# Attention with a token MLP on one core: a planner's settings, a per-window table, ramp jobs with their own priorities, an earlier constant and a scaling in two groups

## The chip, the cores and the metric

The kernel runs on one core of a Trainium2 chip. Its time is device microseconds of that core, taken as the median of several runs. A separate execution was recorded by the hardware profiler; its trace gives a span from the first to the last instruction. Five engines each work through their own list of instructions in order: PE (TensorE, matrix products), ACT (ScalarE), DVE (VectorE), POOL (GpSimd) and SP, which here only starts transfers. Matrix products land in PSUM, 8 banks of 128 x 512 float32.

## The reference

The input x has 2,048 rows of 640 numbers. It is normalised twice: once for the attention, and once more ahead of the MLP.

```python
x = A_x
xn = _layernorm(x)
s = _A_ref(xn, A_wqkv, A_wo)                  # attention, 32 heads of 20
g = _silu(_B_ref(xn, B_w1, B_b1, B_w2, B_b2)) # MLP over the rows (tokens)
return x + s * g

# _A_ref: q, k, v = split(xn @ wqkv); p = softmax(q k^T * 20**-0.5); o = p v; o @ wo
# _B_ref: h = _layernorm(xn); u = gelu(h^T-contraction over rows with w1, 1536 wide, + b1);
#         y = u^T-contraction with w2 (back to 2048) + b2
```

The largest part is the softmax: 32 heads x 2,048 x 2,048 exponentials.

## The kernel before

**Units and passes.** The heads are taken four at a time (eight groups G), the query columns 512 at a time (four blocks). One group and one block make a pass: 16 chunks of 128 keys, four heads each, 64 units of 128 keys x 512 queries. There are 32 passes, the last in two halves. A unit's life: PE makes its scores in a PSUM bank (L1313, four heads side by side in 32-row groups), an engine turns them into weights in SBUF, and PE multiplies the weights with V (L1429), adding to the pass's accumulator bank. The row sums come along as a column of ones in V. When a pass is full, DVE transposes the accumulator (L1557), takes reciprocals (L1560), scales (L1565), and the result goes out by a transfer.

**Two ways to an exponential.** Most units go through ACT: one instruction (L1343) takes two or three banks at once, 128x1024 or 128x1536, and writes bf16 to a ring of 20 slots, pt_sb. The rest go through DVE in tiles of four units (one chunk, four heads). DVE writes an integer whose bits, read as bf16, are a rough exponential (L1354). Three more copies, each with a constant added, are averaged by PE through four differently scaled V operands (v_sb, and vs_sb from L793), which evens the error out. A copy is made by DVE (L1407, 128x2048) or, for the fourth one, by a transfer issued by POOL that adds a constant tile kc_sb onto the first copy in place once PE has used it (L1378). These are the adding transfers. `x_ok` decides between the two, when the third copy is being made:

```python
def x_ok(d):
    if "kc" not in done or pr.xpipe > pr.T["dve"] + self.XQ:
        return False
    return d["q"] > a_cur[0] or a_left(d["q"]) >= self.XLEFT
```

The six banks of ACT form two groups of three. In `do_st`, ACT may lend the third bank of a group to a DVE unit: that exponential then covers two units instead of three. DVE can also use the spare bank 7.

**The planner.** The order is not written by hand. When the program is built, `schedule` plays all engines forward with a cost for each instruction and always emits the ready candidate with the lowest priority number on the engine that can start first. `Prog` keeps the book: `_add` reckons starts, ends and waits, also those of transfers (XISSUE, XMOVE, XTAIL for the adding ones). The result is a fixed list per engine, with waits on semaphores; each list is executed strictly in that order. Class attributes of `_Kern` steer the choices: how much DVE backlog still allows lending (LEND, LENDF), how long a job may wait (LATE, JOBF), the number of ACT units left in a pass below which DVE takes no more (D_GUARD), when an adding transfer is allowed (XLEFT, XQ), where MLP matmuls are spread (MLP_A, MLP_B). `tune` may set them anew every 16 units from the table PLAN and the value lists OPTS; in this kernel PLAN is empty.

**The ramp.** The first 40 to 60 us do what later passes rely on. Rows arrive in blocks of 128 (x), DVE takes statistics two blocks at a time (L557, L559, L564, L568), POOL raises the variance to the power -1/2 (L571), and DVE applies it (L575). The first four blocks are transposed on PE (L626) and evicted by ACT and DVE (L633, L636), the other twelve by transposing transfers from SP (L613). PE then makes k and q of the first group (L660) and V of the first eight heads (L773), evicted by L1140, L1141, L1143 and L1144. The second normalisation is only a further scaling of the same rows: DVE computes its variance from the first (L586, L588, L590), POOL takes a power of 16 columns (L592), and DVE scales all 16 blocks (L595). Bank jobs of the ramp are chosen in `activate_` by readiness and priority. Idle time on PE may be filled with dummy products: L1456 (`emit_warm`) before the first PV product, then L1446 (`emit_fill`), which adds zeros to the accumulator and is drawn only if the planner's own measure of PE's activity is low.

**Around it.** Later q and k are projected in columns of 32 (L675), stored to HBM scratch through three staging slots qs_sb (L705) and loaded back per group (L744). MLP products (L675; row pieces L683 ride beside a score product) and their evictions (L850) fill gaps. At the end the output projection (L992, L997), its product with the gate (L1007, L1775), the residual add (L1033, and for the last two blocks L1777, the first of them on POOL) and the stores (L1042, L1784) remain.

Of the kernel before, what the change touches and what calls it, by code (L numbers as in the profile page):

```python
# [39 lines left out]
class Prog:  # L40
# [7 lines left out]
    XISSUE, XMOVE, XTAIL = 950.0, 2900.0, 4600.0  # L48
# [42 lines left out]
    def _add(self, eng, ceng, fn, reads, writes, name, extra_req=(), cost=100.0, tail=None):  # L91
# [55 lines left out]
        elif ceng not in self.COMPUTE:  # L147
# [3 lines left out]
            if tail is not None:  # L151
                self.T[eng] = start + cost
                self.pipe = max(self.pipe, start) + cost
                t.fin = self.pipe - cost + tail
            else:
                self.T[eng] = start + 450.0
                self.pipe = max(self.pipe, start + 600.0) + cost
                t.fin = self.pipe + (1200.0 if self.pipe < 2500.0 else 2800.0 if cost > 800.0 else 1400.0)
# [125 lines left out]
class _Kern:  # L284
# [16 lines left out]
    D_GUARD = 20  # L301
    MLP_A, MLP_B = 2.6, 24.0
    QK_LEAD = 6.0
    SLACK, MINJ = 0.0, 640.0
    ROOM = 6
    ROWM, ROWP, ROWN = 4, 2, 400
    lastrow = None
    LENDH, LEND1, JLATE = 0.0, 9999.0, 0.0
    LENDF = 1800.0
    MERGE = False  # L310
    OPM = 1
    KLEAD = 300.0
    KPRIO = 22.4
    RAMPEND = ('qk0_1_3', 'qk0_0_1')
    RLEND = 0
    DRDY = 'lnp14'
# [3 lines left out]
    JOBF = 4  # L320
    LONE, DLEAD, DRIDE = True, 0.0, 700.0
# [8 lines left out]
    ACTP = 30.0  # L330
# [3 lines left out]
    OTA, OTD = 24.6, 0.1  # L334
    XLEFT, XQ = 18, 4000.0
# [9 lines left out]
        ("DRIDE", (400.0, 150.0, 700.0)),  # L345
        ("LEND", (1800.0, 1300.0, 2400.0, 700.0, 0.0)),
# [3 lines left out]
        ("LONE", (False, True)),  # L350
# [3 lines left out]
        ("FGAP", (0.0, 40.0, 150.0)),  # L354
# [3 lines left out]
    PLAN = ()  # L358
    PARTS = (3, 1)
# [78 lines left out]
    def schedule(self):  # L438
# [111 lines left out]
        def ln_steps(b0, nb):  # L550
# [10 lines left out]
            for b in bl:  # L561
# [10 lines left out]
                          [sw, S_("mhalf")], sr, f"{nm}pow", 1020.0))  # L572
# [8 lines left out]
        def r2_steps():  # L581
            steps = []
            mvs = [S_(f"mv{b}") for b in range(NB)]
            srs = [S_(f"rstd{b}") for b in range(NB)]
            sw = S_("r2w")
            steps.append(("dve", lambda e: e.tensor_tensor(st(5, 0, NB), st(2, 0, NB), st(2, 0, NB), ALU.mult), srs,  # L586
                          [sw], "r2a", 100.0))
            steps.append(("dve", lambda e: e.tensor_tensor(st(5, 0, NB), st(5, 0, NB), st(1, 0, NB), ALU.mult),  # L588
                          [sw] + mvs, [sw], "r2b", 100.0))
            steps.append(("dve", lambda e: e.tensor_scalar(st(5, 0, NB), st(5, 0, NB), self.EPS, None, ALU.add), [sw],  # L590
                          [sw], "r2c", 100.0))
            steps.append(("pool", lambda e: e.tensor_tensor(st(6, 0, NB), st(5, 0, NB), mhalf(NB), ALU.pow),  # L592
                          [sw, S_("mhalf")], [S_("r2")], "r2d", 2900.0))
            for b in range(NB):
# [157 lines left out]
        def wp_step(w):  # L752
# [3 lines left out]
                     f"wp0_{w}", 430.0),  # L756
                    ("tag", f"wp0_{w}")]

        def v_steps(b, half):
            def make(bk):  # L760
                steps = []
                c0, n = (0, 160) if half == 0 else (160, 480)
# [1511 lines left out]
```

## Time and profile before

| what | value |
|---|---|
| median of 3 runs | 758.12 us (757.94 to 758.52) |
| the profiled execution | 761.36 us, of which span 759.5 us |
| ACT busy | 727.9 us (96%) |
| PE busy | 715.1 us (94%) |
| DVE busy | 684.8 us (90%) |
| POOL busy | 104.6 us (14%) |
| exponentials on ACT (L1343) | 682 |
| adding transfers (L1378) | 94, 512 KB each, median 5.9 us from issue to landing |
| mean granted PE clock | 0.993 |

Busy time counts an instruction from its start to its end. On ACT and DVE a following instruction starts some tenths of a microsecond before the previous one's end, so that a mean duration is longer than the distance between two of them; the busy time of a group counts overlapping stretches once. What follows "|" last in a group is the time its engine stood still just before these instructions, and the work whose end let them start. The clock column shows what share of full speed PE was granted.

### The profile page before, as it was taken

What the parts mean: (1) busy time and instruction counts of PE and PEld (TensorE: products, weight loads), DVE (VectorE), ACT (ScalarE), POOL (GpSimd) and SP (SyncE); (2) the same over time, 40 slices, a digit from 0 to 9 for tenths busy, and PEclk for the clock granted to TensorE, in tenths of its full rate; (3) what the DMA queues carried; (4) which work ended last, traced back from release to release, by engine and by line L of the source; (5) the groups of instructions that cost most, each with busy time, mean ns of one, the idle gap of its engine ahead of it and who ended that gap; (6) DMA issues with size and microseconds to landing.
All of it is one profiled execution on the core that took longest, in us unless ns stands there. A gap on an engine that the chain in (4) does not pass through costs nothing.

```text
span 759.5 us, 23600 instructions
## 1 busy us (share of the span) xinstructions
PE 715.1 (94%) x10485; PEld 240.1 (32%) x10485; DVE 684.8 (90%) x1247; ACT 727.9 (96%) x708; POOL 104.6 (14%) x118
## 2 busy tenths in 40 slices
PE   8889999999999999999999999999999999999997
PEld 7332222222232323233232322332332332332233
DVE  8789889989898988898998898999999999999996
ACT  6879999999999999999999999999999999999994
POOL 4301111011111100000000011120111111001100
PEclk9899999999999999999999999999999999999999
DMA  9749754556787727364313586746679885395522
GB/s 242 139 104 127 152 102 84 104 106 123 140 144 144 151 43 165 79 134 68 68 48 64 117 171 116 149 80 150 121 129 173 150 171 112 63 234 131 107 63 71
DMA packets 133274, 91.95 MB, mean 121 GB/s; under 512 B 80676, under 2 KB 119972, under 8 KB 133124
## 3 DMA queue, kind: packets, MB, share of 16 engines
q0 software_dynamic: 13536, 49.29, 34.9%
q1 hardware_dynamic: 119636, 41.15, 24.9%
q8 instruction: 82, 1.34, 0.7%
q14 instruction: 20, 0.16, 0.1%
HBM read 26.37 MB, written 10.22 MB: 48 GB/s over the span
## 4 chain that ended last, share of the span: by engine, by line
ACT 70%; PE 20%; DVE 6%; DMA 3%; issue 0%; SPq 0%; POOL 0%; DVEq 0%
ACT pt_sb L1343 69%; PE ps_all L1429 6%; PE ps_all L1313 6%; PE ps_all L675 5%; DMA dt_sb<-kc_sb 1%; DVE dt_sb L1354 1%; ACT zt_sb L871 1%; PE ps_all L660 1%; PE ps_all L992 1%; DVE dt_sb L1407 1%; ACT zt_sb L876 1%; DMA regA<-in_A_x_dram 1%; DVE regC L575 1%; DMA xnT_sb<-regC 0%; DVE tr_sb L1557 0%; DVE regC L595 0%
## 5 line engine op out<-in xcount | busy, mean ns | idle before, releaser
L1343 ACT ACTIVATE pt_sb<-ps_all 128x1024 bf16<-128x1024 f32 (+1 forms) x682 | 708.9, 1224 | 10.9 <-PE ps_all L1313 7.5
L1354 DVE TENSOR_SCALAR dt_sb<-ps_all 128x512 uint16<-128x512 f32 x504 | 334.7, 681 | 42.6 <-PE ps_all L1313 20.2
L1313 PE MATMUL ps_all<-qk_sb 32*128 32x512 bf16 (+1 forms) x2128 | 271.1, 377 | 27.7 <-ACT pt_sb L1343 23.4
L1407 DVE TENSOR_SCALAR dt_sb<-dt_sb 128x2048 uint16<-128x2048 uint16 x284 | 186.5, 685 | 2.4 <-PE ps_all L1429 0.4
L1378 POOL DMA_DIRECT2D dt_sb<-kc_sb x94 | 87.5, 944 | 609.3 <-PE ps_all L1429 395.8
L1313 PEld LDWEIGHTS ps_all<-qk_sb 32*128 32x128 bf16 x2128 | 68.5, 91 | 282.4 <-ACT pt_sb L1343 213.6
L1429 PE MATMUL ps_all<-dt_sb,vs_sb 128*21 128x512 bf16 (+1 forms) x1560 | 135.4, 377 | 1.8 <-DMA dt_sb<-kc_sb 1.4
L1429 PE MATMUL ps_all<-pt_sb,v_sb 128*21 128x512 bf16 (+1 forms) x1608 | 127.1, 374 | 3.0 <-DVE v_sb L1141 2.0
L675 PE MATMUL ps_all<-regC,regA 128*32 128x128 bf16 (+1 forms) x1440 | 66.5, 295 | 0.8 <-DVE qs_sb L1141 0.6
L675 PE MATMUL ps_all<-regB,regA 128*32 128x512 bf16 (+1 forms) x1460 | 66.1, 297 | 0.1
L1429 PE MATMUL ps_all<-dt_sb,v_sb 128*21 128x512 bf16 (+1 forms) x520 | 49.6, 376 | 3.4 <-DVE tr_sb L1557 3.2
L1429 PEld LDWEIGHTS ps_all<-dt_sb,vs_sb 128*21 128x21 bf16 x1560 | 35.4, 90 | 54.0 <-issue 30.7
L1429 PEld LDWEIGHTS ps_all<-pt_sb,v_sb 128*21 128x21 bf16 x1608 | 30.6, 90 | 48.8 <-issue 35.7
L675 PE MATMUL ps_all<-xnT_sb,wqk_sb 128*32 128x512 bf16 x612 | 45.3, 382 | 0.0
L683 PE MATMUL ps_all<-regC,regA 32*128 32x512 bf16 x96 | 36.9, 385 | 0.0
L675 PEld LDWEIGHTS ps_all<-regB,regA 128*32 128x32 bf16 x1460 | 27.5, 96 | 24.5 <-issue 12.9
L675 PEld LDWEIGHTS ps_all<-regC,regA 128*32 128x32 bf16 x1440 | 27.1, 96 | 23.3 <-issue 12.0
L683 PE MATMUL ps_all<-regB,regA 32*128 32x512 bf16 x76 | 29.2, 385 | 0.0
L992 PE MATMUL ps_all<-wv_sb,xnT_sb 128*128 128x128 bf16 (+1 forms) x160 | 28.6, 301 | 0.0
L1557 DVE STREAM_TRANSPOSE tr_sb<-ps_all 128x512 f32<-128x512 f32 x31 | 21.9, 707 | 0.9 <-PE ps_all L1429 0.9
L675 PE MATMUL ps_all<-wv_sb,xnT_sb 128*32 128x480 bf16 x312 | 22.2, 384 | 0.0
L1429 PEld LDWEIGHTS ps_all<-dt_sb,v_sb 128*21 128x21 bf16 x520 | 13.2, 91 | 23.9 <-issue 11.1
(93 smaller groups left out, 383.8 us busy)
## 6 DMA issues: line engine op xcount, KB each, us to landing
dt_sb<-kc_sb POOLq DMA_DIRECT2D x94, 512.0 KB, 5.9
regA<-in_B_w_dram SPq DMA_DIRECT2D x6, 1024.0 KB
regA<-in_B_w_dram SPq DMA_DIRECT2D x8, 768.0 KB
qk_sb<-qk_scratch_dram SPq DMA_DIRECT2D x56, 80.0 KB
qk_scratch_dram<-qs_sb SPq DMA_DIRECT2D x32, 128.0 KB
regA<-in_A_x_dram SPq DMA_DIRECT2D x6, 640.0 KB
ok_scratch_dram<-on_sb SPq DMA_DIRECT2D x96, 20.0 KB
out_dram<-regC SPq DMA_DIRECT2D x3, 640.0 KB
```

Of the source, the lines that this page charges most:

```text
L575: steps.append(("dve", lambda e, b=b: e.tensor_scalar(regC[:, b, :], regA[:, b, :], st_sb[:, 0, b:b + 1], st_sb[:, 2, b:b + 1], ALU.subtra ...
L660: steps.append(("pe", lambda e, dc=dc, lhsT=lhsT: e.matmul(ps(bk, n), lhsT, xnT_sb[:, dc, tb * 512 + c0:tb * 512 + c0 + n], start=(dc == 0 ...
L675: fns.append(lambda e, c=c, e_=e_: e.matmul(oc(c, e_), lhsT[:, c:e_], rhs, start=start, stop=stop, tile_position=(0, c)))
L683: row = lambda g: (lambda e: e.matmul(oc(0, 128), lhsT[32 * g:32 * g + 32, :], rhs[32 * g:32 * g + 32, :], start=False, stop=False, tile_p ...
L992: steps.append(("pe", lambda e, c=c: e.matmul(ap, oT_sb[:, c, b * 128:(b + 1) * 128], wo_ap[:, c, c0:c0 + n], start=(opens and c == 0), st ...
L1313: t = pr.pe(lambda e, outp=outp, lhsT=lhsT, rhs=rhs, g=g: e.matmul(outp, lhsT, rhs, start=True, stop=True, tile_position=(32 * g, 0)), rea ...
L1343: tk = pr.act(lambda e: e.activation(outp, inp, AF.Exp, scale=math.log(2.0) / 128.0), reads=[bank_slot[b] for b in banks[:n]], writes=[S_( ...
L1354: tk = pr.dve(lambda e: e.tensor_scalar(w, src, WOFF, 0.0, ALU.add, ALU.max), reads=[bank_slot[bk]], writes=[S_(f"dt{d['tl'][0]}_{g}")], n ...
L1378: t = pr.xdma(lambda e: e.dma_start(dst, kc_sb[:, :, :], accum_op=ALU.add), [S_("kc")] + sl_, sl_, f"dX{d['q']}_{d['c']}")
L1407: tk = pr.dve(lambda e: e.tensor_scalar(dst, src, dk, None, ALU.add), reads=[S_(f"dt{b}_{g}") for b in inb for g in range(4)], writes=[S_( ...
L1429: pr.pe(lambda e: e.matmul(outp, lhsT, rhs, start=(k == 0), stop=last, tile_position=(0, 32 * g)), reads=reads, writes=[bank_slot[AB]], na ...
L1557: steps.append(("dve", lambda e: e.transpose(tr_sb[:, :], ps(AB)), [bank_slot[AB]], [S_("tr")], f"epT{q}", 632.0))
```

## The change

The class attributes are set anew. PLAN gets a table of 122 rows, one for each 16 units, which pick values from OPTS. The reckoned tail of an adding transfer goes from 4.6 to 5.6 us, and every other transfer that starts after 45 us is reckoned 1.5 us longer. The memset of kc_sb loses its requirement, so it is issued ahead of the first power. The second scaling is split into blocks 0 to 7 and 8 to 15. V tiles of the ramp come in groups of one to three blocks (VGRP) with priorities of their own (JP). The residual add of the tail stays on DVE for both last blocks; narrow output products come in pairs (OPM). The diff, with repeated or minor places cut:

```diff
-    XISSUE, XMOVE, XTAIL = 950.0, 2900.0, 4600.0
+    XISSUE, XMOVE, XTAIL = 950.0, 2900.0, 5600.0
...
-                t.fin = self.pipe - cost + tail
+                t.fin = self.pipe - cost + tail + (1500.0 if start > 45000.0 else 0.0)
...
-    D_GUARD = 20
-    MLP_A, MLP_B = 2.6, 24.0
-    QK_LEAD = 6.0
+    D_GUARD = 8
+    MLP_A, MLP_B = 2.0, 25.0
+    QK_LEAD = 7.0
...
-    LENDF = 1800.0
-    OPM = 1
+    LENDF = 2400.0
+    OPM = 2
...
-    RAMPEND = ('qk0_1_3', 'qk0_0_1')
-    RLEND = 0
-    DRDY = 'lnp14'
+    RESP = 39.0
+    R2N = 8
+    XE = ((2,), (2,))
+    JP = {'k0_0': 26.95, 'v0_0': 21.16, 'q0_0': 25.64, 'v0_14': 19.07, 'k0_1a': 25.82, 'v0_13': 30.17, 'v0_8': 19.61}
+    VGRP = ((0, 2), (2, 2), (4, 3), (7, 1), (8, 3), (11, 1), (12, 3), (15, 1))
+    RAMPEND = ('v0_14', 'qk0_0_1')
+    RLEND = 1
+    DRDY = 'qk0_1_3'
...
-    JOBF = 4
-    LONE, DLEAD, DRIDE = True, 0.0, 700.0
+    JOBF = 6
+    LONE, DLEAD, DRIDE = False, 0.0, 700.0
...
-    ACTP = 30.0
+    ACTP = 22.0
...
-    OTA, OTD = 24.6, 0.1
-    XLEFT, XQ = 18, 4000.0
+    OTA, OTD = 25.0, 0.16
+    XLEFT, XQ = 20, 4000.0
...
-    PLAN = ()
-    PARTS = (3, 1)
+    PLAN = (
+        "000000000000000", "000000000000000", "000000000000000", "000000000000000", "100000000000000", "100000000000000",
+        "000030000000000", "000000000000000", "000000000000000", "000030000000000", "000000000000001", "000000000000000",
...
+    )
+    PARTS = (1,)
...
-        def r2_steps():
+        def r2_steps(b0, nb, tag):
...
-            steps.append(("pool", lambda e: e.tensor_tensor(st(6, 0, NB), st(5, 0, NB), mhalf(NB), ALU.pow),
-                          [sw, S_("mhalf")], [S_("r2")], "r2d", 2900.0))
-            for b in range(NB):
+            steps.append(("pool", lambda e: e.tensor_tensor(st(6, b0, nb), st(5, b0, nb), mhalf(nb), ALU.pow),
+                          [sw, S_("mhalf")], [sr], "r2d", 400.0 + 156.0 * nb))
+            for b in bl:
...
-        def v_steps(b, half):
+        def v_steps(b, half, nb=2):
...
-        add_job("r2", r2_steps(), sum((xtag(gb) for gb in range(4)), ()), 43.0)
+        if self.R2N:
+            add_job("r2a", r2_steps(0, self.R2N, "h_a"), sum((xtag(gb) for gb in range((self.R2N + 3) // 4)), ()), 43.0)
+        add_job("r2", r2_steps(self.R2N, NB - self.R2N, "h_all"), (("h_a",) if self.R2N else ()) + sum((xtag(gb) for gb in range(4)), ()), 43.0)
...
         add_job("kc", [("pool", lambda e: e.memset(kc_sb[:, :, :], int(self.DK[3])), [], [S_("kc")], "kc", 1800.0), ("tag", "kc")],
-                ("lnp14",), 43.0)
+                (), 43.0)
...
-            for b in range(4 * gb, 4 * gb + 4, 2):
-                add_bank_job(f"v0_{b}", v_steps(b, 0), xt + ((f"qk0_1_{gb}",) if gb else ("qk0_0_0", "qk0_1_0")), self.VPRIO + gb)
+            for b, nb in self.VGRP:
+                if (b + nb - 1) // 4 == gb:
+                    need = xt + (xtag(gb - 1) if b // 4 < gb else ())
+                    add_bank_job(f"v0_{b}", v_steps(b, 0, nb), need + ((f"qk0_1_{gb}",) if gb else ("qk0_0_0", "qk0_1_0")), self.VPRIO + gb)
...
-            steps.append(("pool" if i < 1 else "dve", lambda e: e.tensor_tensor(g0, g0, regA[:, b, 0:512], ALU.add),
+            steps.append(("dve", lambda e: e.tensor_tensor(g0, g0, regA[:, b, 0:512], ALU.add),
...
-                  (80.0 if pr.T["pe"] < 4500.0 else 0.0), w=81.0)
+                  (80.0 if pr.T["pe"] < 5600.0 else 0.0), w=81.0)
...
-                        c.append((99.0, max(T, 1000.0), emit_warm))
+                        c.append((99.0, max(T, 1185.0), emit_warm))
```

## The prediction

> **What bounds the kernel now.** I read four views in this order. First the page's engine row.
>
> ```profile
> PE 715.1 (94%) x10485; PEld 240.1 (32%) x10485; DVE 684.8 (90%) x1247; ACT 727.9 (96%) x708; POOL 104.6 (14%) x118
> ```
>
> Busy times of pipelined work include tails, so PE at 94% is not yet the bound. ACT has 759.5 - 727.9 = 31.6 us without work; DVE has 74.7. Second, the chain of work that ended last (70% of it runs through ACT), and busy time by stretch, which tells where those 31.6 us lie:
>
> ```profile
> ACT 70%; PE 20%; DVE 6%; DMA 3%; issue 0%; SPq 0%; POOL 0%; DVEq 0%
> ```
>
> ```profile
> 0.00:20.00 20.00, 17.48 (x202) 14.23 (x206) 17.02 (x63) 12.06 (x16) 8.40 (x16) 1.00 0.94 236
> 20.00:40.00 20.00, 17.55 (x148) 6.08 (x141) 13.94 (x45) 15.53 (x12) 6.88 (x6) 0.83 0.76 155
> 40.00:60.00 20.00, 17.85 (x199) 6.69 (x197) 17.80 (x41) 17.23 (x18) 2.56 (x2) 1.00 0.42 94
> 60.00:100.00 40.00, 37.94 (x496) 11.00 (x488) 34.23 (x61) 37.19 (x37) 3.70 (x5) 0.96 0.77 129
> 100.00:150.00 50.00, 49.44 (x675) 14.34 (x671) 48.13 (x83) 49.93 (x51) 7.52 (x8) 1.00 0.53 99
> ...
> 500.00:550.00 50.00, 47.24 (x747) 15.03 (x744) 49.09 (x87) 49.38 (x51) 5.99 (x8) 1.00 0.60 120
> ...
> 740.00:759.50 19.50, 13.99 (x201) 6.77 (x201) 13.51 (x29) 8.63 (x8) 1.15 (x1) 0.99 0.20 69
> ```
>
> Columns: length; PE, PEld, DVE, ACT, POOL busy with counts; granted clock; DMA share; GB/s. ACT misses 15.2 us before 60 (7.9 + 4.5 + 2.8), 2.8 from 60 to 100, about 2.7 from 100 to 740, and 10.9 at the end. So from 60 to 740 the time is ACT's queue of exponentials, back to back, and a change pays in two ways: less in that queue, or less idle at the start, at 90-97 and at the end.
>
> Third, the costliest groups with shapes kept apart: the prices.
>
> ```profile
> L1343 ACT ACTIVATE pt_sb<-ps_all 128x1024 bf16<-128x1024 f32 x500 | 483.8, 1115 | 3.7 <-PE ps_all L1313 2.7 <-PE ps_all L683 0.2
> L1354 DVE TENSOR_SCALAR dt_sb<-ps_all 128x512 uint16<-128x512 f32 x504 | 334.7, 681 | 42.6 <-PE ps_all L1313 20.2 <-PE ps_all L683 19.2
> L1343 ACT ACTIVATE pt_sb<-ps_all 128x1536 bf16<-128x1536 f32 x181 | 265.7, 1531 | 7.2 <-PE ps_all L1313 4.8 <-PE ps_all L1429 2.2
> L1407 DVE TENSOR_SCALAR dt_sb<-dt_sb 128x2048 uint16<-128x2048 uint16 x284 | 186.5, 685 | 2.4 <-PE ps_all L1429 0.4
> L1378 POOL DMA_DIRECT2D dt_sb<-kc_sb x94 | 87.5, 944 | 609.3 <-PE ps_all L1429 395.8 <-DVE dt_sb L1407 127.9 <-DVE zt_sb L850 21.6
> ```
>
> Fourth, the timeline of the places where ACT stood: around 28 us, and near the end.
>
> ```profile
> 28.13 1.81 POOL L1611 MEMSET kc_sb<- 128x2048 uint16 x1
> 28.22 1.90 DVE L575 TENSOR_SCALAR regC<-regA,st_sb 128x640 bf16<-128x640 bf16 x1 [0.81 <-POOL st_sb L571]
> ...
> 752.73 1.15 POOL L1777 TENSOR_TENSOR regC<-regC,regA 128x512 bf16<-128x512 bf16 x1 [20.51 <-DVE regC L1775]
> 752.87 1.35 DVE L1033 TENSOR_TENSOR regC<-regC,regA 128x640 bf16<-128x640 bf16 x1
> ```
>
> Twice a DVE instruction that alone takes 0.4 to 0.5 us ran as long as a POOL instruction beside it.
>
> **The change, part by part.** A planner writes every queue's order when the program is built, so the built instruction lists of both kernels tell what moved; no time is taken from the planner.
>
> *The mix of units.* A unit is one 128x512 block of scores. ACT's exponentials go from 500 of two units, 181 of three and 1 of one (1,544 units) to 514 and 168 (1,532). There are 682 instructions both times, so only columns go: 12 x (1,531 - 1,115 = 416 ns) = **-5.0 us** on the queue that sets 60 to 740. The 12 units move to DVE: 12 x 334.7/504 = 8.0 us. The adding transfers (L1378) fall from 94 to 64, so L1407 rises from 284 to 323: 39 x 186.5/284 = 25.6 us. Other DVE edits nearly cancel: 7 products of 256 columns for 14 of 128 save about 0.7, one residual add comes from POOL for 0.4, V evictions 0.4 more. DVE goes from 684.8 to about 718 us. In 60 to 740 it has 57.4 us free (680 less the sum of its stretches), so this lies beside ACT with some 24 left; a DVE stall then delays a borrowed bank (L1354), hence the score matmuls, hence ACT. The stretches 100-150 and 500-550 show DVE at 48.1 and 49.1 of 50 while ACT lost 0.1 and 0.6. Scaled from the latter, 680 us at such density lose 8.4; from the former, 1.0. I take **+1.5**, since only some stretches become so dense.
>
> *PE.* 56 more column pieces, 48 more matmuls with DVE weights, 12 fewer with ACT's and 36 fewer zero fillers are 56/4 = 14 more passes of four; a pass adds 0.22 us (groups of 8 span 0.61, of 4 span 0.39): 3.1 us, against 44 without work. The 56 row pieces that vanish started with a score matmul and cost nothing. PE: 0.
>
> *The constant.* The memset of kc_sb goes from behind the last of the eight power instructions to ahead of the first, behind v_ones, which ends at 2.76 + 2.85 = 5.61. POOL's first power (5.86, 0.72 long) now waits until 5.6 + 1.8 = 7.4, so DVE's first L575, at 6.92 today, starts at 8.1; behind it wait the 20 transposes on PE, the first projections and the first exponential (11.01). **+1.2 us** at the start, unhidden. In return the 1.90 us L575 becomes 0.4, and 0.8 of waiting around it shrinks.
>
> *Ramp jobs and second scaling.* V evictions get groups and priorities; 8 of the 16 scalings (L595, 0.3 us apart) move ahead of the last V work. DVE's list up to the last L575 carries 0.9 us more work and 1.2 of late start, and sheds the 1.5 at 28.2 and about 1.2 of waits. It comes out even, but ten scalings no longer stand in one block (39.19 to 42.2) ahead of a V eviction, for which PE, the exponential buffers and ACT waited. ACT's waits between 30 and 44 are 1.05 + 0.56 + 2.72 + 2.21 = 6.5 us. Bounds: 0 regained, or all 6.5; I take **-4**, because the list puts nearly every V eviction before the second group. The second power (128x16: 2.90; 128x2: 0.69, so 128x8 about 1.6) stands ahead of two first powers, but 2.6 us of DVE work stand before the next apply: hidden by 0.2; without that cover it costs at most 1.6.
>
> *A rule against this part: the clock.* In the ramp's first pass fillers drop from 60 matmuls to 24. The clock stood at half from 32.2 to 39.1 and from 93.7 to 97.1:
>
> ```profile
> 28.80:32.20 3.40, 2.06 (x19) 0.71 (x17) 3.10 (x10) 3.15 (x3) 1.61 (x2) 1.00 0.39 78
> 32.20:39.06 6.86, 6.71 (x29) 1.53 (x29) 2.48 (x8) 4.24 (x3) 2.57 (x2) 0.50 0.89 235
> 90.30:93.70 3.40, 2.19 (x25) 0.58 (x22) 1.64 (x3) 2.24 (x3) 0.00 (x0) 1.00 0.39 132
> 93.70:97.10 3.40, 3.40 (x32) 0.85 (x31) 2.85 (x7) 2.06 (x2) 0.00 (x0) 0.50 0.43 129
> ```
>
> The Trainium skill (TensorE: Matmul & The Clock Gate, HAM oscillation) puts it as no PE-idle gap above about 3.4 us. By that, no gap here (longest 1.21) would drop the clock, and fewer fillers cost 0. The rows disagree: a window of 3.4 us with 2.06 or 2.19 us of mostly narrow matmuls was enough (as in the page's next section, on a kernel with many short idles). So 36 fillers x 53 ns (a quarter of a 0.22 us pass) = 1.9 us less activity over the ramp may cost another half-clock window, about 1.5 us of ACT as at 93.7. I go by the rows, but a ramp with fewer waits is also denser: 0 in the sum, +1.5 to +3 in the range.
>
> *Transfers reckoned longer.* The planner now adds 1.5 us to transfers after 45 us. That spreads work away from landings such as this one:
>
> ```profile
> DVE qs_sb L1144 <- DMA qk_scratch_dram<-qs_sb: 1.8, 1, 1.8
> ```
>
> At 90.3 DVE stood 1.80 us on it, two L1354 behind it and PE 1.21 for those; then came the half clock; ACT lost 1.28 + 1.22 = 2.5. I take **-2.2** (bounds 0 and -2.5).
>
> *End.* The residual add leaves POOL, so the 1.35 us L1033 falls to 0.48 and one add of 0.43 joins DVE; the last two stores no longer issue together (0.4). Against it, DVE's list has 3 units' work between the last scores and the last transpose, perhaps 1 us later. **-0.5** (-1.5 to +1).
>
> *Sum:* -5.0 + 1.5 + 1.2 - 4 - 2.2 - 0.5 = -9.0, thus 750.5 of span. The profiled execution took 761.36 for its 759.5; the runs' median is 758.12, 3.2 below it. I carry that offset over: 758.12 - 9.0 = **749.1**.
>
> **Rivals.** (a) *DVE becomes the bound* (slower). DVE's idle of 74.7 was 39.4 us of L1354 waiting for scores, 17 at the two ends, and small waits. With 33 us more work it may keep at most 41 idle. If only half the 57.4 inside 60 to 740 goes, DVE ends 28.7 - 24.4 = 4.3 late: 758.1 + 4.3 = 762.4; beyond half of the waits kept, it decides. The two dense stretches speak against it. (b) *The ramp gains nothing*, late start and another clock window eat it: -5.0 + 1.5 + 1.2 - 2.2 + 1.5 = -3.0: 755. (c) *Longer reckoning does nothing*, since the landings were hidden anyway: PE waited on adding transfers for 1.4 us in all. With the ramp even: -5.0 + 1.5 + 1.2 + 2 of new stalls, 758. (d) *More goes*: the ramp's 6.5 in full, no denser stalls: 744.5.
>
> **How the numbers follow.** Main case 0.55 (own range 746 to 753), (a) 0.12, (b) 0.15, (c) 0.05, (d) 0.13. Range 743.5 to 757: it leaves out (a), half of (c) and a little of (d). A difference under 0.2% (1.5 us) is about what a measurement of this kernel cannot tell from none. Faster by more: 0.55 + 0.15 + 0.13 = 0.83; within: 0.05; slower: 0.12.
>
> **What would show it.** ACT busy near 723 and DVE near 718; the first exponential at about 12.2; no 1.90 us apply; ACT's waits from 30 to 44 under 3; clock at 1.00 from 90 to 97; ACT idle from 100 to 740 under 5. Wrong if ACT's idle inside 100 to 740 exceeds 10 us, or the half clock lasts longer in the ramp.

## The result and the profile after

| | before | after |
|---|---|---|
| median of the runs | 758.14 us (757.94 to 758.52) | **745.36 us** (744.40 to 745.93) |
| profiled execution, and its span | 761.36, 759.5 | 745.50, 743.6 |
| mean granted TensorE clock in the profile | 0.993 | 1.000 |

The ratio is 0.983, with a 95% interval of 0.9812 to 0.9847: 12.8 us faster, against 9.0 predicted. The spans differ by 15.9, since the profiled execution of before was 3.2 us slower than its median, and that of after only 0.1.

The page of after, its engine row and the chain that ended last:

```profile
PE 706.2 (95%) x10472; PEld 238.1 (32%) x10486; DVE 706.5 (95%) x1295; ACT 721.9 (97%) x708; POOL 74.9 (10%) x88
ACT 71%; PE 21%; DVE 4%; DMA 3%; issue 1%; SPq 0%; POOL 0%
```

ACT is busy for 6.0 us less than before and DVE for 21.7 more, in a span 15.9 shorter. ACT's time without work falls from 31.6 to 21.7. Where it fell is seen in busy time by stretch of after (length; PE, PEld, DVE, ACT, POOL busy with counts; granted clock; DMA share; GB/s):

```profile
0.00:20.00 20.00, 16.58 (x190) 13.62 (x191) 16.70 (x57) 11.13 (x15) 10.16 (x17) 1.00 0.88 231
20.00:40.00 20.00, 17.91 (x178) 7.42 (x176) 17.99 (x68) 19.35 (x18) 5.71 (x6) 1.00 0.81 162
40.00:60.00 20.00, 18.64 (x201) 6.11 (x203) 19.77 (x39) 19.44 (x21) 1.93 (x2) 1.00 0.67 127
60.00:100.00 40.00, 39.31 (x530) 11.35 (x522) 36.93 (x66) 39.81 (x39) 3.46 (x4) 1.00 0.59 99
100.00:150.00 50.00, 48.43 (x666) 14.13 (x663) 46.56 (x77) 49.95 (x50) 3.67 (x5) 1.00 0.42 81
500.00:550.00 50.00, 48.42 (x824) 16.30 (x820) 47.20 (x83) 49.80 (x51) 5.72 (x6) 1.00 0.60 124
725.00:743.60 18.60, 14.14 (x216) 7.45 (x217) 15.46 (x34) 9.81 (x9) 0.00 (x0) 1.00 0.21 72
```

The length less ACT's busy time is what ACT missed. From 20 to 40 us it missed 4.5 us before and 0.65 now; from 40 to 60, 2.8 and 0.56; from 60 to 100, 2.8 and 0.19; at the end 10.9 and 8.8. Only the start is worse, 7.9 and 8.9. With the 6.0 us of busy time that is -6.0 + 0.9 - 3.8 - 2.2 - 2.6 - 2.1 = -15.8, the difference of the spans. Between 100 us and the last stretch ACT missed 2.7 us before and 2.6 now.

The groups with shapes kept apart, after (busy us, mean ns of one; idle time ahead of them and what ended it):

```profile
L1373 ACT ACTIVATE pt_sb<-ps_all 128x1024 bf16<-128x1024 f32 x514 | 498.0, 1124 | 1.9 <-PE ps_all L1343 1.0 <-PE ps_all L713 0.2
L1373 ACT ACTIVATE pt_sb<-ps_all 128x1536 bf16<-128x1536 f32 x168 | 250.5, 1543 | 3.0 <-PE ps_all L1343 2.4 <-PE ps_all L1459 0.3
...
L1384 DVE TENSOR_SCALAR dt_sb<-ps_all 128x512 uint16<-128x512 f32 x516 | 343.0, 683 | 20.9 <-PE ps_all L1343 14.5 <-PE ps_all L713 4.2
L1437 DVE TENSOR_SCALAR dt_sb<-dt_sb 128x2048 uint16<-128x2048 uint16 x323 | 212.0, 688 | 1.6
...
L1408 POOL DMA_DIRECT2D dt_sb<-kc_sb x64 | 58.4, 912 | 608.0 <-PE ps_all L1459 338.2 <-DVE dt_sb L1437 194.4 <-DVE on_sb L1595 37.1
```

The two DVE groups grew by 8.3 and 25.5 us, against 8.0 and 25.6 forecast. DVE's waits for scores, the two releasers shown in its first row, fell from 39.4 to 18.7: the new work went into them.

### The profile page after: what moved, and what is told of

Same layout as the page of the kernel before. It is cut to its first block, busy times and chain, and to the rows that moved or that the text cites. A ratio compares the mean times of both kernels' runs of the same rounds, so it can differ in the third digit from the quotient of the medians.

```text
span 743.6 us, 23596 instructions
## 1 busy us (share of the span) xinstructions
PE 706.2 (95%) x10472; PEld 238.1 (32%) x10486; DVE 706.5 (95%) x1295; ACT 721.9 (97%) x708; POOL 74.9 (10%) x88
## 4 chain that ended last, share of the span: by engine, by line
ACT 71%; PE 21%; DVE 4%; DMA 3%; issue 1%; SPq 0%; POOL 0%
ACT pt_sb L1373 69%; PE ps_all L1459 7%; PE ps_all L1343 6%; PE ps_all L705 6%; DMA dt_sb<-kc_sb 1%; DVE dt_sb L1384 1%; ACT zt_sb L906 1%; DMA bload_sb<-in_B_b_dram 1%; DVE dt_sb L1437 1%; ACT zt_sb L901 1%; PE ps_all L1022 1%; PE ps_all L690 0%; DMA regA<-in_A_x_dram 0%; SPq L1626 0%; DVE qk_sb L1174 0%
## 5 line engine op out<-in xcount | busy, mean ns | idle before, releaser
L1373 ACT ACTIVATE pt_sb<-ps_all 128x1024 bf16<-128x1024 f32 (+1 forms) x682 | 703.5, 1227 | 4.9 <-PE ps_all L1343 3.5
L1384 DVE TENSOR_SCALAR dt_sb<-ps_all 128x512 uint16<-128x512 f32 x516 | 343.0, 683 | 20.9 <-PE ps_all L1343 14.5
L1437 DVE TENSOR_SCALAR dt_sb<-dt_sb 128x2048 uint16<-128x2048 uint16 x323 | 212.0, 688 | 1.6
L1408 POOL DMA_DIRECT2D dt_sb<-kc_sb x64 | 58.4, 912 | 608.0 <-PE ps_all L1459 338.2
L705 PE MATMUL ps_all<-regB,regA 128*32 128x128 bf16 (+1 forms) x1476 | 67.7, 297 | 0.0
L705 PE MATMUL ps_all<-xnT_sb,wqk_sb 128*32 128x512 bf16 x640 | 47.7, 382 | 0.2 <-DVE qs_sb L1171 0.2
L705 PEld LDWEIGHTS ps_all<-regC,regA 128*32 128x32 bf16 x1444 | 27.1, 96 | 23.8 <-issue 12.8
L1022 PE MATMUL ps_all<-wv_sb,xnT_sb 128*128 128x128 bf16 (+1 forms) x150 | 25.6, 295 | 1.4 <-issue 1.4
L713 PE MATMUL ps_all<-regB,regA 32*128 32x512 bf16 x60 | 23.1, 385 | 0.0
L705 PEld LDWEIGHTS ps_all<-xnT_sb,wqk_sb 128*32 128x32 bf16 x640 | 13.6, 95 | 19.2 <-issue 8.8
```

What stands on the lines that cost most here:

```text
L705: fns.append(lambda e, c=c, e_=e_: e.matmul(oc(c, e_), lhsT[:, c:e_], rhs, start=start, stop=stop, tile_position=(0, c)))
L713: row = lambda g: (lambda e: e.matmul(oc(0, 128), lhsT[32 * g:32 * g + 32, :], rhs[32 * g:32 * g + 32, :], start=False, stop=False, tile_p ...
L1022: steps.append(("pe", lambda e, c=c: e.matmul(ap, oT_sb[:, c, b * 128:(b + 1) * 128], wo_ap[:, c, c0:c0 + n], start=(opens and c == 0), st ...
L1373: tk = pr.act(lambda e: e.activation(outp, inp, AF.Exp, scale=math.log(2.0) / 128.0), reads=[bank_slot[b] for b in banks[:n]], writes=[S_( ...
L1384: tk = pr.dve(lambda e: e.tensor_scalar(w, src, WOFF, 0.0, ALU.add, ALU.max), reads=[bank_slot[bk]], writes=[S_(f"dt{d['tl'][0]}_{g}")], n ...
L1408: t = pr.xdma(lambda e: e.dma_start(dst, kc_sb[:, :, :], accum_op=ALU.add), [S_("kc")] + sl_, sl_, f"dX{d['q']}_{d['c']}")
```

## The experiments

A caution for all of them: the planner lays down every queue anew when one setting changes. Where an experiment says "fixed order", the finished lists were kept and one instruction was moved or put in; all others are new plans. Because executions differ by the clock (next part), the table also has a mean at full clock: each run less 0.67 us for each 0.001 that its mean granted clock lies below 1. The 0.67 was fitted to the kernel before; for the other kernels it is an estimate.

| kernel | median us | ratio to the kernel before beside it (95%) | mean clock | mean at full clock |
|---|---|---|---|---|
| before, 56 executions beside the others (medians 759.8, 757.8, 760.0 in three sets) | 759.6 | | 0.9965 | 757.2 |
| after, 4 executions | 745.4 | 0.983 (0.981, 0.985) | 0.9995 | 744.9 |
| b_fill | 761.2 | 1.003 (1.001, 1.004) | 0.9955 | 758.3 |
| b_kcearly | 758.6 | 0.998 (0.996, 1.000) | 0.9969 | 756.2 |
| b_tail, 11 of 12 executions (the other: 770.6 at a clock of 0.982) | 761.9 | 1.002 (1.000, 1.004) | 0.9946 | 757.6 |
| b_xfer | 763.5 | 1.005 (1.003, 1.008) | 0.9962 | 761.2 |
| b_ramp | 771.2 | 1.014 (1.010, 1.018) | 0.9915 | 764.8 |
| b_dvemore | 776.3 | 1.022 (1.018, 1.026) | 0.9952 | 774.3 |
| a_kclate | 745.4 | 0.983 (0.980, 0.986) | 0.9995 | 745.3 |
| a_kcdve | 745.5 | 0.983 (0.980, 0.986) | 0.9978 | 744.2 |
| a_noplan | 749.0 | 0.987 (0.984, 0.990) | 0.9998 | 748.8 |
| a_tailold | 752.5 | 0.990 (0.987, 0.992) | 0.9973 | 750.9 |
| a_xold | 770.6 | 1.014 (1.010, 1.019) | 0.9942 | 767.3 |
| a_dvemore | 776.3 | 1.023 (1.020, 1.026) | 0.9990 | 775.4 |

### What the clock has to do with it

**b_fill** (before, fixed order): eight matmuls by zeros in each of two pauses of PE.

```diff
+        for i in (958, 257):            # places in PE's list: 92.3 us and 29.7 us
+            for k in range(8):
+                q.insert(i, matmul(accumulator rows of group k % 4, zw_sb, wp_sb, start=False, stop=False))
```

> The kernel before in its own order, with eight matmuls by zeros more in each of two gaps of TensorE, at 29.7 us and at 92.3 us, where TensorE waited 0.86 and 1.21 us and nothing else is moved. Theory 1 (what share of a 3.41 us window TensorE works decides on the clock of the next): the half clock at 32 to 39 us and at 93.7 to 97.1 us is gone, and ScalarE waits 1 to 3 us less in these two places: 755.5 to 757. Theory 2 (the half clock does not depend on so little work, or costs nothing since scores stand ready ahead of ScalarE): the half clock stays, or goes without effect, 758.1 within 0.4.

The half clock was gone from both places, and then stood at 228.8 us, a place that had run at full clock before (stretches of b_fill, columns as above):

```profile
225.39:228.80 3.41, 1.78 (x26) 0.65 (x30) 1.72 (x4) 1.46 (x2) 0.00 (x0) 1.00 0.13 29
228.80:232.21 3.41, 3.41 (x29) 0.55 (x21) 2.48 (x5) 2.69 (x4) 0.00 (x0) 0.50 0.00 0
```

The mean clock was no better, and the time was 1.4 us longer by the medians. The profiled run shows no wait that the fills caused; that rest is unexplained. Theory 1 fails as a remedy.

The reason came out of all runs together. The 56 executions of the kernel before had mean clocks from 0.990 to 1.000 and times from 756.5 to 763.9 us; the fit is 757.2 + 0.67 us for each 0.001 lost (correlation -0.86). In b_kcearly the half clock stood at 90.6 us, in b_tail at 678 and 740, with the same work around 30 us at full clock. In each of the 14 traces the changes lie whole multiples of 3.413 us apart (32.2 and 93.7: 18.0 of them), and this grid starts elsewhere in each execution (its first change lies between 4.05 and 6.93 us). The Trainium skill (TensorE: Matmul & The Clock Gate, Part 1: The HAM clock gate) says the same of its window: 3,413 ns long, and free-running.

Laid over the traces, the grid has 14 falls to half clock while PE still had work. In the window ahead of 13 of them PE was busy for 0.39 to 2.42 of the 3.41 us, which puts them among the six emptiest of the 216 to 225 windows of their traces; in the last one (b_tail, 736.4 us) for 2.71. A long pause is not needed: in 13 of the 14 the longest was 0.29 to 3.20 us. And a thin window is not enough, since others, one of 1.64 us among them (b_ramp, 449 us), were followed by full clock. So the fall depends on how the grid cuts PE's work into windows, and only in part on how busy PE is in one of them; what else decides stays open.

What three such windows cost is read from two traces of the same order. One group of exponentials, before:

```profile
529.82 5.12 ACT L1343 ACTIVATE pt_sb<-ps_all 128x1536 bf16<-128x1536 f32 x5 [0.42 <-PE ps_all L1313]
```

and the same in b_tail, which up to there ran at full clock:

```profile
525.61 5.12 ACT L1344 ACTIVATE pt_sb<-ps_all 128x1536 bf16<-128x1536 f32 x5 [0.42 <-PE ps_all L1314]
```

4.2 us earlier, though its first exponential came 0.5 later (11.50 against 11.01): 4.7 us for three windows, 1.6 each. The fit gives 1.5, since one window takes 0.00225 from the mean clock. The four runs of the kernel after had 1.000, 1.000, 0.998, 1.000. PE stood still for 37.4 us of its span, against 44.4 before; that this is why it loses less clock is likely, but not shown.

### One part alone, in the kernel before

**b_kcearly** (fixed order):

```diff
-POOL: ... ln14pow, kc, ...
+POOL: ... v_ones, kc, ln0pow, ...
```

> The kernel before in its own order; only the constant's fill on GpSimd is moved from behind the eighth power to ahead of the first. Theory 1 (it delays the first power, and all that is behind it, by about 1.2 us, and nothing is won later, since what follows the eighth power has slack): first exp at 12.2 us instead of 11.0, 758.6 to 759.3. Theory 2 (the late fill was in the way of VectorE at 33 us, where one apply took 1.90 us): the apply is normal again, about 0.4 us, and the time falls by 0.5 to 1.5: 756.6 to 757.6.

758.6 against 759.8 in the runs beside it, 756.2 against 757.2 at full clock: about 1 us faster. The later start of theory 1 and the gain of theory 2 were both true. The first exponential came at 12.08, the apply took 0.45 us again, and ACT missed 3.2 us from 30 to 44 us, against 4.2 in b_tail, which has the late fill and full clock there. The start itself varies: in the traces with the late fill the first exponential came at 11.0 to 12.0 us, in those with the early one at 12.1 to 12.4.

**b_tail**:

```diff
-    OPM = 1                                   # and the residual's priority 30.0
+    OPM = 2                                   # and 39.0
-            steps = [... ("pool" if i < 1 else "dve", lambda e: e.tensor_tensor(g0, g0, regA...
+            steps = [... ("dve", lambda e: e.tensor_tensor(g0, g0, regA...
```

> The kernel before with the edits of the end alone (output projections two blocks in one job, the residual's priority, the last residual additions on VectorE). The order is the same as before up to the last of the 32 passes. Theory 1 (what the two traces show at the end, ScalarE idle 10.87 against 8.79 us, belongs to these edits): 756.0. Theory 2 (as predicted, 0.5 us): 757.6. Theory 3 (the end is bound by the last epilogue and its stores, which these edits leave as they are): 758.1 within 0.3.

No gain is shown. Two half-clock windows in the profiled run fell into the end itself (739.8 to 746.6), so its waits there say little. From the last exponential to the end of the span it took 10.3 us, against 10.9 before: 0.6, about as predicted, and no more.

**b_xfer**:

```diff
-    XISSUE, XMOVE, XTAIL = 950.0, 2900.0, 4600.0
+    XISSUE, XMOVE, XTAIL = 950.0, 2900.0, 5600.0
```

(and 1,500 ns on transfers after 45 us, as in the change)

> The kernel before with only the transfers reckoned longer, planned anew. The order that comes out has 12 more ScalarE units than before (1,556) and 492 adding units on VectorE. Theory 1 (units cost 0.416 us each, and the longer reckoning takes away the wait of some 1 us at 91 us and no more): 759.5 + 5.0 - 1 = 763.5. Theory 2 (the longer reckoning alone takes away waits spread over the whole of the units): below 759. Theory 3 (an order made with longer transfers only adds units and waits): above 765.

763.5, as theory 1 has it, though not for its whole reason. The page's engine row of b_xfer:

```profile
PE 712.4 (94%) x10497; PEld 241.5 (32%) x10513; DVE 671.2 (88%) x1228; ACT 732.5 (96%) x709; POOL 102.5 (13%) x116
```

ACT is 4.6 us busier than before for 12 units, 0.39 each. The wait at 91 us went, but ACT's missed time from 60 to 100 us was 0.97, against 0.83 in b_tail at full clock: smaller waits took its place. So alone the longer reckoning saved nothing, and the time at full clock grew by 3.9.

**b_ramp**:

```diff
+    R2N = 8; JP = {...}; VGRP = (...)
-    RAMPEND = ('qk0_1_3', 'qk0_0_1'); RLEND = 0; DRDY = 'lnp14'
+    RAMPEND = ('v0_14', 'qk0_0_1');   RLEND = 1; DRDY = 'qk0_1_3'
-    ... "kc" requires ("lnp14",)
+    ... "kc" requires ()
```

> The kernel before with the edits of the ramp alone (constant early, the jobs' own priorities, groups of the value jobs, second scaling in two groups, the ramp's end), planned anew, all later settings as before. The order that comes out has 12 more ScalarE units than before (1,556 against 1,544; 492 adding units on VectorE in place of 504). Theory 1 (a unit costs ScalarE 0.416 us, and the ramp's edits take away the waits between 20 and 60 us): 758.1 + 5.0 for the units + 0.9 for the later first exp - 6.0 for the waits = 758.0; ScalarE idle between 20 and 60 us under 2 us. Theory 2 (the count of units decides nothing, only the ramp does): 753.0. Theory 3 (the ramp's waits went through the later settings, not through the ramp's edits): ScalarE idle between 20 and 60 us stays near 7 us, and the time is 764.

Slower than all three theories. The ramp itself did what was hoped; stretches of b_ramp:

```profile
20.00:40.00 20.00, 17.98 (x174) 7.41 (x171) 16.93 (x66) 19.26 (x17) 5.70 (x6) 1.00 0.80 162
...
60.00:100.00 40.00, 38.30 (x517) 11.34 (x514) 35.92 (x65) 39.68 (x39) 3.65 (x4) 1.00 0.55 99
600.00:650.00 50.00, 41.33 (x649) 13.61 (x641) 32.90 (x55) 39.13 (x39) 4.35 (x5) 0.86 0.87 126
```

ACT misses 0.7 us from 20 to 40 and 0.3 from 60 to 100, nearly as in after. But the new plan has 12 more ACT units (ACT 733.7 busy, +5.8), and misses 10.9 us between 600 and 650. There the load of the MLP's weights stood on SP's list behind twelve transposing transfers, and PE could use it only 16 us after its issue, with four more of them issued meanwhile; PE waited for it in order, and ACT for PE (4.45 us). Three windows of half clock followed (612.8 to 623.0); in them PE stood 2.35 us more, for nothing that the trace shows, ahead of ACT's second wait of 3.34. The timeline of b_ramp (SP, PE, ACT):

```profile
574.35 23.85 SPq L969 DMA_TRANSPOSE xnT_sb<-ok_scratch_dram  x12
598.29 0.53 SPq L824 DMA_DIRECT2D regA<-in_B_w_dram  x1
598.87 17.53 SPq L969 DMA_TRANSPOSE xnT_sb<-ok_scratch_dram  x4
...
614.45 2.75 PE L682 MATMUL ps_all<-regB,regA 128*32 128x512 bf16 x24 [3.20 <-DMA regA<-in_B_w_dram]
...
617.78 1.02 ACT L1350 ACTIVATE pt_sb<-ps_all 128x1024 bf16<-128x1024 f32 x1 [4.45 <-PE ps_all L690]
622.15 15.98 ACT L1350 ACTIVATE pt_sb<-ps_all 128x1024 bf16<-128x1024 f32 x15 [3.34 <-PE ps_all L690]
```

The ramp, the transfers and the end, each alone, thus give +7.6, +3.9 and +0.4 us at full clock (the constant, which b_ramp has too, -1.0); the whole change gives -12.3.

### One part taken out of the kernel after

**a_xold**: the reckoning of transfers as before, all else as after.

```diff
-    XISSUE, XMOVE, XTAIL = 950.0, 2900.0, 5600.0
+    XISSUE, XMOVE, XTAIL = 950.0, 2900.0, 4600.0
```

(and without the 1,500 ns)

> The kernel after with the transfers reckoned as short as before, all else kept, planned anew (the table of stretches was made for the other reckoning). The order that comes out has 28 more ScalarE units (1,560 against 1,532; 488 adding units on VectorE in place of 516). Theory 1 (a unit costs ScalarE 0.416 us, and waits for transfers come back here and there): 745.4 + 11.6 + 1 to 5 = 758 to 762. Theory 2 (VectorE is as much the bound as ScalarE, so that 28 adding units less, at 1.05 us each, give back what ScalarE pays): 745 to 750. Theory 3 (the wait seen where the ramp alone was changed, 11 us for weights that came late behind the transposing transfers, comes back): 768 or more.

25 us slower than after, 22 at full clock. That is the number of theory 3, but not its wait: between 600 and 650 us ACT missed 0.2 us. ACT is busy 735.3 us, 13.4 more, for 28 units (0.48 each). The rest is 11.8 us of waits; the largest is in the timeline of a_xold:

```profile
725.06 0.39 PE L1022 MATMUL ps_all<-wv_sb,xnT_sb 128*128 128x512 bf16 x1 [3.61 <-DMA xnT_sb<-oT_scratch_dram]
...
727.40 2.10 ACT L1373 ACTIVATE pt_sb<-ps_all 128x1024 bf16<-128x1024 f32 x2 [4.17 <-PE ps_all L1343]
```

A matmul laid down for a transfer that had not landed held PE for 3.6 us, and ACT stood 4.2, the last part of it at half clock (from 725.5 us). It is the kind of wait that the longer reckoning is meant to prevent. Theory 2 is out. How much is owed to the table, which was made for the other reckoning, this run cannot tell.

**a_tailold**: the edits of the end undone.

```diff
-    OPM = 2                                   # and the residual's priority 39.0
+    OPM = 1                                   # and 30.0; first last-block residual on POOL again
```

> The kernel after with the edits of the end undone; the order is the same up to the last passes. Theory 1 (the edits of the end give nothing, as where they were made alone in the kernel before): 745.4 within 0.7. Theory 2 (they give 1.5 to 2 us in the order after, where ScalarE's last stretch is shorter): 747 to 747.5.

7 us slower, more than either theory, against nothing for the same edits in the kernel before. The order is that of after up to the last passes, and the last exponential ends at the same time (735.0 against 734.8). The stretch behind it, and its timeline, in a_tailold:

```profile
735.00:751.00 16.00, 8.09 (x84) 3.94 (x84) 9.33 (x19) 0.04 (x1) 1.15 (x1) 0.82 0.19 65
```

```profile
735.05 0.69 DVE L1037 TENSOR_TENSOR regC<-ps_all,regC 128x512 bf16<-128x512 f32 x1 [1.24 <-PE ps_all L1027]
...
740.07 0.39 PE L1343 MATMUL ps_all<-qk_sb 32*128 32x256 bf16 x2 [0.39 <-DVE regC L1037]
...
743.64 0.45 DVE L1579 STREAM_TRANSPOSE tr_sb<-ps_all 128x256 f32<-128x256 f32 x1 [0.53 <-PE ps_all L1459]
```

Output projections of finished blocks (L1022, L1027, evicted by L1037) stand ahead of the last two scores and hold the banks. So the last pass's transpose comes at 743.64, where after has it at 736.19, and 15.9 us follow the last exponential in place of 8.8. In after:

```profile
736.19 0.45 DVE L1579 STREAM_TRANSPOSE tr_sb<-ps_all 128x256 f32<-128x256 f32 x1 [0.55 <-PE ps_all L1459]
```

The half clock that a_tailold shows from 745.4 us on is not the cause: from this transpose to the end it takes 7.25 us there and 7.44 in after. So the 7 us by the medians are the better figure here than the 6.0 at full clock.

What is worth nothing in one order decides the end of another.

**a_noplan**: the table of stretches empty; same counts of all units, another order from 40 us on.

```diff
-    PLAN = ("000000000000000", ... )
+    PLAN = ()
```

> The kernel after with the table of settings by stretch left empty, so that each stretch is planned with the class's own settings. The order differs from 40 us on, but the counts are the same: 1,532 ScalarE units, 516 adding units on VectorE, 323 second halves, 108 matmuls by zeros. Theory 1 (the number of units carries the gain): 745 to 747. Theory 2 (the table's order hides waits that the plain order shows): 749 or more, with ScalarE idle between 60 and 700 us up by 4 us.

749.0: 3.6 us slower than after, past theory 1 and at the edge of theory 2, but not where theory 2 had it. ACT's busy time is the same (721.8). The stretch from 60 to 100 us in a_noplan:

```profile
60.00:100.00 40.00, 38.67 (x518) 11.39 (x518) 37.88 (x69) 38.59 (x39) 2.61 (x3) 1.00 0.58 96
```

1.4 us missed in place of 0.2, and 11.1 us behind the last exponential in place of 8.8. From 100 to 700 us ACT missed 3.0 us, against 2.6. So the table gives 3.6 us by order alone.

**a_kclate** (fixed order): the fill of kc_sb back behind the eighth power.

```diff
-POOL: ... v_ones, kc, ln0pow, ...
+POOL: ... ln14pow, kc, ...
```

> The kernel after in its own order; only the constant's fill is moved back behind the eighth power. Theory 1 (the early fill costs the start 0.9 to 1.2 us, and the late place costs VectorE one apply of 1.90 us at 30 us, which has slack): first exp near 11.1 us, 744.3. Theory 2 (in the denser ramp the late fill stands in the way of VectorE's applies and of the adding units from 37.8 us on): 745.4 to 747.

745.35 against 745.36: no difference, and both mechanisms are in the trace. After has the early fill, with DVE and POOL around it:

```profile
5.36 1.96 POOL L1643 MEMSET kc_sb<- 128x2048 uint16 x1
7.43 1.59 POOL L600 TENSOR_TENSOR st_sb<-st_sb,cst_sb 128x2 f32<-128x2 f32 x2
...
5.79 1.56 DVE L597 TENSOR_SCALAR st_sb<-st_sb 128x2 f32<-128x2 f32 x1
...
12.37 1.44 ACT L1373 ACTIVATE pt_sb<-ps_all 128x1536 bf16<-128x1536 f32 x1
```

a_kclate starts earlier and has its fill later:

```profile
11.40 1.45 ACT L1381 ACTIVATE pt_sb<-ps_all 128x1536 bf16<-128x1536 f32 x1
...
28.15 1.83 POOL L1651 MEMSET kc_sb<- 128x2048 uint16 x1
28.39 2.13 DVE L612 TENSOR_SCALAR regC<-regA,st_sb 128x640 bf16<-128x640 bf16 x2
```

Of the microsecond won at the start, about half is lost behind 28 us, where two applies take 2.13 us (0.80 for two elsewhere in the same trace): ACT missed 1.0 us from 30 to 44, against 0.3. The rest is spread over small waits and busy time later on.

### How much room VectorE has

**a_dvemore** and **b_dvemore** (fixed order): a small fill of scratch on DVE behind each second half of an adding unit.

```diff
 DVE: ... dT (the 128x2048 copy with a constant), ...
+DVE: ... dT, memset(dum_sb[...32 partitions, 2 elements]), ...
```

> The kernel after in its own order, with a small fill of scratch (some 72 ns) on VectorE after each of its 323 second halves of an adding unit: 23 us more work on VectorE, spread over the whole of the units. It computes nothing that is used. Theory 1 (ScalarE is the bound at 722 us busy, VectorE has slack): under 753, and 745.4 if all 23 us fall into idle time. Theory 2 (with 706 us busy VectorE already binds as much as ScalarE): the time grows by most of the 23 us, 763 to 769.

776.3: 30.9 us slower than after. The fill's group in a_dvemore, its engine row and its chain:

```profile
L469 DVE MEMSET dum_sb<- 32x1 uint32 x323 | 19.1, 59 | 11.3
```

```profile
PE 735.6 (95%) x10486; PEld 247.5 (32%) x10486; DVE 736.0 (95%) x1618; ACT 734.7 (95%) x708; POOL 75.1 (10%) x88
DVE 49%; PE 33%; ACT 10%; issue 6%; DMA 2%; SPq 0%; POOL 0%; DVEq 0%
```

19.1 + 11.3 = 30.4 us of DVE's list were added, 94 ns for each fill where the expectation had 72, and all of it appears. Theory 1 is wrong. The chain that ended last went over from ACT (71%) to DVE (49%). The row also warns against reading busy time as work: with the same exponentials and matrix products, ACT is busy 12.8 us longer than in after and PE 29.4. Records that follow each other at once overlap and count once; where an engine waits more, they overlap less (ACT's durations add up to 862.4 us in after and to 804.4 here).

> The kernel before in its own order, with the same small fill of scratch on VectorE after each of its 284 second halves of an adding unit. In the kernel after such a fill took 94 ns of VectorE (59 busy, 35 ahead of it), and 323 of them took 30.8 us of the time. Theory 1 (the kernel before left VectorE slack: 685 us busy of 758, 39 us of its waits were for TensorE's tiles, and the change uses that slack up): of the 26.7 us under 15 appear, 766 to 774. Theory 2 (in an order laid down ahead each VectorE instruction costs its time in either kernel): 783 to 787.

776.3 against 760.0 beside it: 16.3 us for 16.8 + 9.8 = 26.6 put in (17.1 at full clock). That lies between the theories, nearer to the first one's 15: the kernel before took up 10 of 26.6 us, the kernel after none of 30.4. The change has used up the room that DVE had, in these two orders.

### A version that might beat both

**a_kcdve** (fixed order): the fill on DVE, ahead of the first input.

```diff
-POOL: ... v_ones, kc, ln0pow, ...
+DVE:  ... zw, kc, ...
```

> The kernel after in its own order; the constant's fill is done on VectorE, behind its first small fill, where VectorE is idle from 1.2 to 3.1 us, and GpSimd has nothing ahead of the powers. By VectorE's fills in this trace (72 ns for 16 words, 272 ns for 256) it takes some 0.9 us. Theory 1 (the early fill on GpSimd costs 1.2 us in the start): first exp near 11.1 us, 744.2. Theory 2 (the start is made up later, since the ramp is set by the loads of the input): 745.4 within 0.4.

The powers start at 5.94 again, but in the profiled run the start was no earlier. DVE and PE of a_kcdve:

```profile
1.53 1.76 DVE L1654 MEMSET kc_sb<- 128x2048 uint16 x1 [0.37 <-issue]
...
8.91 0.49 DVE L597 BATCH_NORM_STATS2 bst_sb<-regA 128x6 f32<-128x320 bf16 x1 [1.11 <-DMA regA<-in_A_x_dram]
...
10.14 0.61 PE L701 MATMUL ps_all<-xnT_sb,wp_sb 128*128 128x256 bf16 x4 [1.23 <-DVE xnT_sb L677]
```

The fill took 1.76 us, not the 0.9 reckoned. That hardly delayed the start; in this trace it was delayed by a block of input rows, for which DVE's list stood 1.11 us, ahead of an apply and of the copies that PE needs for the first projection. In a_kclate the same instruction started at 7.93, here at 8.91, and the first exponential was at 12.38. That is the reason that theory 2 gives, the loads of the input, and also its number: the medians are equal (745.54). At full clock it is 0.8 us better than after, but three of its six runs lost clock (0.995, 0.995, 0.997), so no gain is shown.

## Why the prediction was right, and where its terms were off

The direction, the range and the main mechanism held; 745.36 lies 3.7 us under the forecast and just under the main case's own range of 746 to 753. The number is that of rival (d), more goes, whose terms add up to 745.1 and not to the 744.5 written: no denser stalls came true, but of the ramp's 6.5 us only about 4 were there to be had at full clock. ACT's busy time (721.9, about 723 forecast), its idle time between 100 us and the last stretch (2.6, under 5 forecast) and the full clock from 90 to 97 us came out as said. To judge the terms, the half clock is taken out of before by using b_tail's trace, which has the order of before and full clock until 678 us. Its stretches:

```profile
0.00:20.00 20.00, 17.63 (x198) 14.54 (x198) 16.72 (x59) 11.89 (x15) 8.40 (x16) 1.00 0.91 233
20.00:40.00 20.00, 17.11 (x179) 6.98 (x176) 16.54 (x56) 15.86 (x13) 6.88 (x6) 1.00 0.76 153
40.00:60.00 20.00, 17.85 (x205) 6.18 (x197) 17.80 (x38) 18.95 (x19) 3.27 (x3) 1.00 0.53 109
60.00:100.00 40.00, 38.62 (x520) 11.43 (x516) 36.23 (x65) 39.17 (x39) 3.86 (x5) 1.00 0.72 124
```

| step | predicted | measured, full clock | from |
|---|---|---|---|
| 12 ACT units | -5.0 | -6.0 | ACT busy 727.9 to 721.9 |
| denser DVE | +1.5 | 0 | missed time from 100 us on unchanged, about 2.6 |
| start | +1.2 | +0.8 | 8.1 to 8.9 missed up to 20 us |
| ramp | -4.0 | -4.0 | 4.1 + 1.05 to 0.65 + 0.56 missed, 20 to 60 us |
| transfers reckoned longer | -2.2 | -0.6 | 0.83 to 0.19 missed, 60 to 100 us |
| end | -0.5 | -2.1 | 10.9 to 8.8 behind the last exponential |
| sum | -9.0 | -11.9 | means at full clock: -12.3 |

Part of the agreement is luck. The two terms missed worst, transfers by 1.6 us and the end by 1.6, cancel. And the -4 for the ramp was a choice between 0 and 6.5, where the 6.5 held half clock that the medians hardly have.

**The units.** The step held: the exponentials alone are busy for 5.4 us less (708.9 to 703.5), and the other 0.6 is more overlap with ACT's other records, not less work. The price of a unit, 0.42 us, fits the 0.39 of b_xfer and the 0.48 of a_xold, as closely as busy time can show it.

**DVE.** This is the term whose size came out small for a reason that the prediction did not have. It treated the 24 us left as room of which dense stretches lose a little. The groups grew by the 33.8 us reckoned, yet the engine row by 21.7 only (the forecast was 718, the page says 706.5): records of instructions that follow at once overlap, and they do so more here, since the durations of all DVE records add up to 764.7 before and 803.3 after. At this load nothing is lost; but a_dvemore shows that in this order no room is left: 94 ns more at 323 places come through in full, as rival (a), DVE as the bound, would have it. It did not come about, since this plan asks of DVE no more than it can do. How a smaller addition would fare was not tried.

**Start and ramp.** The first exponential came at 12.37 (12.2 forecast), the 1.90 us apply is gone, and ACT missed 0.3 us from 30 to 44 (under 3 forecast). That the ramp's edits do this is shown by b_ramp. But b_kcearly and a_kclate show the constant's place to be no loss: early, it was 1 us faster in the kernel before, and made no difference in the kernel after. So "+1.2, unhidden" was about right at the start (0.8), and what the late fill cost, which the prediction put into the ramp's term, was worth as much.

**Transfers.** The mis-sized step. The 2.5 us lost near 91 us were in about equal parts a landing waited for (1.28) and a half-clock window (1.22). At full clock the wait near 91 us costs ACT 0.5 to 0.7 us (b_tail 0.68, b_fill 0.73, b_dvemore 0.50); only b_kcearly has half clock there again. So 0.6 was to be had. And alone the step gives nothing (b_xfer). Its worth lies in the new order, where the old reckoning makes 28 more ACT units and 11.8 us of waits: 22 us at full clock in a_xold. Rival (c), longer reckoning does nothing, is right of the kernel before and wrong of the one after.

**End.** Mis-sized likewise: 0.6 is what the edits give in the old order (10.9 to 10.3), 7 us what they are worth in the new one.

**The clock.** 0 in the sum was wrong for the pair of profiles, where 4.7 of 15.9 us are half clock that after does not have. For the medians it was nearly right, since the runs of before that they compare were, by the fit, near full clock (758.1 against 757.2). The offset of 3.2 us that the prediction carried over from the profiled execution was this clock: the terms at 30 to 40 and 90 to 97 us and the offset held the same loss, once each, so part of it was counted twice. The worry that fewer fillers cost another window was not borne out.

**What stays open.** Which of the settings for the later stretches brings about the plan with 516 adding units: of the parts tried alone, none does, and two bring fewer (492 in b_ramp and in b_xfer). Taken out of the new kernel, the longer reckoning is needed (488 without it), the table and the edits of the end are not. Whether 30 fewer adding transfers gain anything of their own, beside the 25.5 us that they cost DVE, was not tried either. The settings D_GUARD, MLP_A, ROWM, ACTP and the rest were not tried by themselves.

## What to carry to other kernels

When a planner lays down all queues, the parts of a change don't add up: test a part by taking it out of the new version as well as by putting it into the old one, and expect the two to differ, here 7 against 0. An engine with idle time in the totals may have no room: put a known small cost into its list and see how much of it reaches the end. Before a difference of a few microseconds is explained, plot the runs against their granted clock, and take one window of half clock as a cost that the next run may not pay.

## What the runs showed of the hardware that was not expected

- The same program's mean granted clock went from 0.990 to 1.000 over 56 executions, and over 29 of them on one chip as well; in the traces the half-clock windows of 3.41 us stood at changing places; each cost 1.5 to 1.6 us, close to the 1.7 us of work that PE loses in it.
- A GpSimd fill of 128x2048 (1.8 to 2.0 us) stretched single DVE instructions beside it: a 128x2 scaling from 0.15 to 1.56 us, two 128x640 applies from 0.80 to 2.13.
- The same fill on DVE took 1.76 us. Two other DVE fills in that trace took 72 ns for 16 elements of 4 bytes and 272 ns for 256, or 0.83 ns for each more; at that rate 2,048 elements of 2 bytes make an estimated 1.76. So the fill went by elements, and the 0.9 of the expectation had counted bytes.
- A DVE fill of two elements took 59 ns and opened 35 ns ahead of it: 94 ns of list for almost no work.
- A block of input rows landed up to 1 us later in one execution than in another: the DVE instruction that needs it started at 7.86 us in before, 8.27 in b_tail and 8.91 in a_kcdve, and the first exponential came at 11.01, 11.50 and 12.38.
